# Where the matrix engine's tiles begin in memory, and the order of the first two units' products

## The chip, the cores and the metric

The kernel runs on one core of one Trainium2 chip. The metric is the device time of one execution in microseconds (us), the median of 3 runs. TensorE (PE) multiplies, VectorE (DVE), ScalarE (ACT) and GpSimd (POOL) do the elementwise work, SyncE (SP) issues the transfers. PEld is TensorE's weight load, which runs beside its matmuls.

## The reference

Attention with a sigmoid in place of the softmax, then two feed-forward layers (the "mixtures"):

```
scores = scale * q @ k.T - log(S);  attn = 1 / (1 + exp(-scores));  x = attn @ v
x = reshape(x)                                  # 1792 tokens x 768
h = x @ w_in;  x = (h * cos(h)) @ w_out         # 768 -> 2048 -> 768
g = x @ w_gate;  v = x @ w_val                  # 768 -> 1536 each
out = (silu(g) * v) @ w_out2                    # 1536 -> 768
```

Four batches, 12 heads, 448 positions, head size 64. The weights come in as 64-bit floats.

## The kernel before

Everything is held transposed: 128 partitions are features, the free dimension is tokens, 448 at a time. Each operand of a mixture's product is split in two parts, a rounded one (`fp32r`) and what the rounding left, and a product is three matmuls, part by part (`THREE`).

**Attention** (`attention`, 24 pairs of heads): 24 matmuls for the scores (line 732), a sigmoid on ACT, 16 for the weighted values (line 746). Beside it the first weights are turned from 64-bit words to floats.

**The mixtures** are worked in units: a half of the tokens (`NH` = 2) by two blocks of 128 columns of the hidden layer. A unit has one sum of products in layer 1 and two (gate and value) in layer 2, 40 in all. Each such sum is seven products instead of eight (a Strassen-like form, `seven`), numbered 1 to 7; each is 9 matmuls of a 128x128 weight block with a 128x448 moving block (line 998). Then come the unit's down products: 6 steps of 12 matmuls (line 900). So there are 40 x 7 x 9 = 2520 up matmuls and 28 x 72 = 2016 down matmuls, 4536 in all. Layer 1 has 16 units (1008 up, 1152 down), layer 2 has 12 (1512 up, 864 down).

The order of the products is a string of tokens for each unit (lines 256 to 266): a digit is a product, `d` a down step of the unit before. `tokens(n, u)` hands it out. Product 1 opens a bank `a`; ACT copies it to bank `b` (`first_copy`, line 927); 6 adds into `a` and 2 into `b` after that; a second copy of `a`, after 6, goes to bank `e` (`second_copy`, line 932), and 7 and 3 wait for it.

The operands and their tiles:

- moving, up: `X[1], X[5], X[2], X[6]` stand in the tile `x0` (line 202), `X[7], X[3], X[4]` in `x1` (line 400), which takes the place of a pool that the attention had. `x0` and `x1` both read as `x` in the profile.
- moving, down: `g0` to `g3` (line 1062).
- weights: pairs of blocks `wa0, wa1` (line 215), `wb0` to `wb2` (line 1060) and one pair at the end of `x1` (line 402; in the profile it reads as `x` too), and single blocks `s` (line 216).

A moving block is 448 x 4 = 1792 bytes of a partition and a weight block 512; both are whole multiples of 128. So where a tile begins, counted past a multiple of 128 bytes, every block in it begins. In the built program these are: `x0` 0, `x1` 96, `g` 64, weights 64, the pair in `x1` 96. Attention's tiles begin at 64, `t` (the ring of raw weights) at 0, `u` (temporaries) at 64.

The order of the instructions on all engines is set by a planner in the kernel (`Order`, lines 74 to 147): each step has an assumed duration and a due time that comes from the token strings (lines 301 to 326), and the planner writes the steps down engine by engine. At run time every engine takes its list strictly in order.

Quoted lines:

```
THREE = ((0, 0), (0, 1), (1, 0))
FIRST = "1526734"
ONE = ("1526dd7d3d4dd", "15d2d6d7d3d4d")
TWO = "15d26d73d4"
```

Of the kernel before, what the change touches and what calls it, by code (L numbers as in the profile page):

```python
# [9 lines left out]
F32 = mybir.dt.float32  # L10
F32R = mybir.dt.float32r
# [139 lines left out]
def block_kernel(  # L151
# [12 lines left out]
    P = 128  # L164
# [6 lines left out]
    KH = KD // 2  # L171
# [2 lines left out]
    assert T == NH * 2 * N and B == 2 * NH and NP == KD and KD % 2 == 0  # L174
    NF1 = w_in.shape[0]
    NF2 = w_gate.shape[0]
    THREE = ((0, 0), (0, 1), (1, 0))
    ADD, SUB = ALU.add, ALU.subtract

# [7 lines left out]
    xp = ctx.enter_context(tc.tile_pool(name="xp", bufs=1))  # L187
# [7 lines left out]
    size, WT = KH * 2 * N, KD * P  # L195
    X = {}

    def give_x(tile, numbers):
        for a, i in enumerate(numbers):
            X[i] = tile[:, a * size:(a + 1) * size].rearrange("p (k m t) -> p k m t", k=KH, m=2)  # L200

    give_x(xp.tile([P, 4 * size], F32R, tag="x0", name="x0"), ORDER[:4])
    ring = xp.tile([P, 3, WT], F32, tag="t", name="t")
    sums = xp.tile([P, W], F32, tag="sum", name="sum")
    warm = xp.tile([P, 16], F32, tag="warm", name="warm")
    order = Order()
    free_t, raws, convs, pairs, singles, gslots, tmps, rounds, downbanks = (Slots(order) for _ in range(9))
    for a in range(2):
# [2 lines left out]
    def make_pairs(pool, n, name):  # L211
        for i in range(n):
            pairs.give(pool.tile([P, 2, 2, KH, P], F32R, tag=f"w{name}{i}", name=f"w{name}{i}"))
# [28 lines left out]

    NC = {1: NF1 // 2, 2: NF2 // 2}
    units = [(layer, h, c) for layer in (1, 2) for h in range(NH) for c in range(NC[layer])]
# [8 lines left out]

    PRODUCT = 0.203

    FIRST = "1526734"
    ONE = ("1526dd7d3d4dd", "15d2d6d7d3d4d")
    TWO = "15d26d73d4"
    LAST = ('1526d734', '15d26d73d4dd')

    def tokens(n, u):
        if n == 0:
            return FIRST
        if n == n_units - 1:
            return LAST[u]
        return TWO if units[n][0] == 2 else ONE[units[n - 1][2] % 2]
# [75 lines left out]
    scratch, ended = {}, []  # L342
    for w, n in ((w_in, NF1), (w_out, NF1), (w_gate, NF2), (w_val, NF2), (w_out2, NF2)):
        for f in range(n):
# [1 line left out]
            if w.dtype != U64:  # L346
                scratch[id(w), f][1].set()

    def stashed(n):
        return False  # L350

    def needs():

        def downs(n):
            if not (units[n][1] and stashed(n)):
                for k in range(2):
                    yield [(w_out if units[n][0] == 1 else w_out2, 2 * units[n][2], i, k) for i in range(2)]

        for n, (layer, h, c) in enumerate(units):
            if not (h and stashed(n)):  # L360
                for w in (w_in,) if layer == 1 else (w_gate, w_val):
                    for i in range(2):
                        yield [(w, 2 * c, i, None)]
                    if n and w in (w_in, w_gate):
                        yield from downs(n - 1)
            elif n:
                yield from downs(n - 1)
        yield from downs(n_units - 1)
# [17 lines left out]
    def lend_pool():  # L386

        pool = tc.tile_pool(name="ln", bufs=1, side="right")
        ln, stop, backs = pool.__enter__(), [], []
        for a in range(4):  # L390
            raw = ln.tile([P, WT, 2], I32, tag=f"lr{a}", name=f"lr{a}")
            t = ln.tile([P, WT], F32, tag=f"lt{a}", name=f"lt{a}")
            backs.append(order.event())
            order.spawn(conversions(raw, t, backs[-1], stop), end)

        def swap():
            assert all(back.time is not None for back in backs)
            pool.__exit__(None, None, None)
            xr = ctx.enter_context(tc.tile_pool(name="xr", bufs=1, side="right"))
            x1 = xr.tile([P, 3 * size + 2 * WT], F32R, tag="x1", name="x1")  # L400
            give_x(x1, ORDER[4:])
            pairs.give(x1[:, 3 * size:].rearrange("p (m a k c) -> p m a k c", m=2, a=2, k=KH))
            x_open.set()

        return stop, swap
# [98 lines left out]
    def operands():  # L504
# [32 lines left out]
                stash[at][1].set()  # L537

        def stash_of(keys):
            n = keys[0][1] if keys[0][0] == "d" else keys[0][0]  # L540
            layer, h, c = units[n]
            return h, stashed(n), (layer, c) + (keys[0][2:] if keys[0][0] != "d" else ("d", *keys[0][2:]))

        def again(keys, size):

            room = pairs if size == WT else singles
            s = yield room
            there, event = stash[stash_of(keys)[2]]
            yield event
            yield move(f32(s), there)  # L550
            done = order.event()
            users[id(s)] = len(keys)
            order.spawn(here(keys, s, room, done), 4)
# [21 lines left out]

        def downs(n):
            for k in range(2):
                if units[n][1] and stashed(n):
                    yield from again([("d", n, i, k) for i in range(2)], WT)
                else:  # L580
                    yield from down(n, k)

        def late(n):
            return tokens(n, 0).index("6") < tokens(n, 0).index("d")

        last_sums = None
        for n in range(n_units):
            if units[n][1] and stashed(n):
                yield from again([(n, 0, 1), (n, 0, 2)], WT)
                yield from again([(n, 0, 5)], W)  # L590
                if not late(n):
                    yield from downs(n - 1)
                yield from again([(n, 0, 6), (n, 0, 3)], WT)
                if late(n):
                    yield from downs(n - 1)
                yield from again([(n, 0, 7), (n, 0, 4)], WT)
                continue
            for u in range(units[n][0]):
                a0 = yield from take()
                a1 = yield from take()  # L600
                a11, a12, a21, a22 = a0[:, :W], a0[:, W:], a1[:, :W], a1[:, W:]
                first = yield from split([(n, u, 1), (n, u, 2)], a0)
                if last_sums:
                    yield last_sums
                yield combine(sums, a21, a22, ADD, due[n, u, 5] - 3.0)
                yield combine(a21, a11, a21, SUB, due[n, u, 7] - 3.0)
                last_sums = yield from split([(n, u, 5)], sums)
                yield first
                yield combine(a11, sums, a11, SUB, due[n, u, 6] - 4.0)
                yield combine(a12, a12, a11, SUB, due[n, u, 3] - 4.0)  # L610
                if n and u == 0 and not late(n):
                    yield from downs(n - 1)
                yield from split([(n, u, 6), (n, u, 3)], a0, a0)
                if n and u == 0 and late(n):
                    yield from downs(n - 1)
                yield from split([(n, u, 7), (n, u, 4)], a1, a1)
# [70 lines left out]
    def attention():  # L687
        with tc.tile_pool(name="at", bufs=2) as at:
# [36 lines left out]
            def scores(i, c):  # L725
# [3 lines left out]
                sc = banks[:, first:first + 2, :S]  # L729
                for n, (m, p) in enumerate(THREE):  # L730
                    for j, half in enumerate(heads):
# [147 lines left out]
    def down(n):  # L879
# [4 lines left out]
        for at, (j, d) in enumerate(steps):  # L884
# [10 lines left out]
            def do(_):  # L895
                for e in range(d, d + 2):
                    for i in range(2):
                        w, g = operand(("d", n, i, e // KH)), gs[n, i, j]
                        for m, p in THREE:
                            nc.tensor.matmul(  # L900
# [18 lines left out]
    def seven(n, u, turn, z, downs):  # L919
# [55 lines left out]
        for token in tokens(n, u):  # L975
# [18 lines left out]
            def do(_, i=i, bank=bank):  # L994
                w, x = operand((n, u, i)), X[i]
                for k in range(KH):
                    for m, p in THREE:
                        nc.tensor.matmul(  # L998
# [47 lines left out]
    with tc.manual_schedule():  # L1046
        nc.gpsimd.memset(warm, 0.0)
        for s in range(n_stages):
            order.spawn(inputs(s), 3.5)
        order.spawn(loads(), 3)  # L1050
        order.spawn(operands(), 4)
        order.spawn(banker(), 2)
        attention()
        with tc.tile_pool(name="mp", bufs=1) as mp:
            for i in range(2):
                raws.give(mp.tile([P, WT, 2], I32, tag=f"raw{i}", name=f"raw{i}"))
                order.spawn(conversions(), end)
            convs.give(mp.tile([P, WT], F32, tag="cv", name="cv"))
            convs.give(ring[:, 2])
            make_pairs(mp, 3, "b")  # L1060
            for i in range(4):
                gslots.give(mp.tile([P, 2, N], F32R, tag=f"g{i}", name=f"g{i}"))
            for i in range(6):
                (tmps if i < 5 else rounds).give(mp.tile([P, N], F32, tag=f"u{i}", name=f"u{i}"))
            free_t.give(mp.tile([P, WT], F32, tag="t3", name="t3"))
            order.spawn(tensor_engine(), 0)
            order.run()
            assert not order.open
# [51 lines left out]
```

## Time and profile before

| | |
|---|---|
| time, median of 3 runs | 1100.19 us (1099.14 to 1101.25) |
| the profiled execution's own time | 1099.62 us |
| its span | 1097.8 us |
| instructions | 14763 |
| PE busy | 1080.3 us, 98% |
| PEld busy | 933.7 us, 85% |
| DVE busy | 849.6 us, 77% |
| ACT busy | 663.5 us, 60% |
| POOL busy | 126.4 us, 12% |
| DMA | 156.68 MB, mean 143 GB/s |

The profiled execution took 1099.62 us, of which 1.8 lie around the span. Busy time of PE says little of how fast it goes: a matmul's record lasts longer than the distance to the next one. What a matmul costs is the distance of the starts. In the timeline a row is a group of alike instructions; the start of the next row less its own start, over the count, is the mean distance.

### The profile page before, as it was taken

What the parts mean: (1) busy time and instruction counts of PE and PEld (TensorE: products, weight loads), DVE (VectorE), ACT (ScalarE), POOL (GpSimd) and SP (SyncE); (2) the same over time, 40 slices, a digit from 0 to 9 for tenths busy, and PEclk for the clock granted to TensorE, in tenths of its full rate; (3) what the DMA queues carried; (4) which work ended last, traced back from release to release, by engine and by line L of the source; (5) the groups of instructions that cost most, each with busy time, mean ns of one, the idle gap of its engine ahead of it and who ended that gap; (6) DMA issues with size and microseconds to landing.
All of it is one profiled execution on the core that took longest, in us unless ns stands there. A gap on an engine that the chain in (4) does not pass through costs nothing.

```text
span 1097.8 us, 14763 instructions
## 1 busy us (share of the span) xinstructions
PE 1080.3 (98%) x5507; PEld 933.7 (85%) x5507; DVE 849.6 (77%) x1139; ACT 663.5 (60%) x1002; POOL 126.4 (12%) x99
## 2 busy tenths in 40 slices
PE   9999999999999899999998999999999999999998
PEld 5555569999998799999997999999999999999997
DVE  4979759888999988988899888887559634655643
ACT  6888768776777777777776565544335444433330
POOL 0100001111211101100023111111111110110100
PEclk9999999999999999999998999999999999999999
DMA  9999334455644155544514566555122322212002
GB/s 268 303 284 234 120 116 148 170 181 185 222 162 139 45 188 187 187 144 158 179 52 144 177 207 212 179 193 168 37 65 75 133 66 73 59 43 72 29 1 101
DMA packets 64455, 156.68 MB, mean 143 GB/s; under 512 B 10112, under 2 KB 36736, under 8 KB 64384
## 3 DMA queue, kind: packets, MB, share of 16 engines
q1 hardware_dynamic: 64240, 155.51, 44.3%
q8 instruction: 43, 0.70, 0.3%
q10 hardware_dynamic: 144, 0.23, 0.1%
q14 instruction: 28, 0.23, 0.1%
HBM read 123.47 MB, written 32.24 MB: 142 GB/s over the span
## 4 chain that ended last, share of the span: by engine, by line
PE 89%; DVE 8%; ACT 1%; issue 1%; DMA 0%; DVEq 0%; ACTq 0%
PE banks L998 42%; PE banks L900 34%; PE banks L746 7%; PE banks L732 6%; DVE r L228 2%; DVE x L228 2%; DVE u L228 1%; DVE g L228 1%; DVE wb L228 1%; DVE u L814 1%; DMA rqk<-in_qk 0%; DVE wa L228 0%; ACT u L225 0%; DVE t L433 0%; DVE x L658 0%
## 5 line engine op out<-in xcount | busy, mean ns | idle before, releaser
L900 PE MATMUL banks<-g,wb 128*128 128x448 f32 x1044 | 228.5, 367 | 0.5 <-DVE g L228 0.4
L998 PE MATMUL banks<-x,wb 128*128 128x448 f32 x1044 | 228.9, 367 | 0.0
L998 PEld LDWEIGHTS banks<-x,wb 128*128 128x128 f32 x1044 | 197.2, 189 | 17.4 <-ACT banks L225 0.3
L900 PEld LDWEIGHTS banks<-g,wb 128*128 128x128 f32 x1044 | 196.0, 188 | 18.3 <-DVE g L228 1.1
L900 PE MATMUL banks<-g,wa 128*128 128x448 f32 x720 | 162.7, 373 | 9.8 <-ACT g L225 8.0
L998 PE MATMUL banks<-x,wa 128*128 128x448 f32 x738 | 162.7, 367 | 0.0
L900 PEld LDWEIGHTS banks<-g,wa 128*128 128x128 f32 x720 | 137.4, 191 | 23.7 <-ACT g L225 9.2
L998 PEld LDWEIGHTS banks<-x,wa 128*128 128x128 f32 x738 | 138.5, 188 | 13.0 <-issue 0.7
L225 ACT ACTIVATE u<-u 128x448 f32<-128x448 f32 x179 | 99.8, 571 | 44.2 <-DVE u L228 26.8
L228 DVE TENSOR_TENSOR u<-u,banks 128x448 f32<-128x448 f32 x119 | 73.3, 617 | 65.5 <-PE banks L998 60.5
L228 DVE TENSOR_TENSOR r<-banks,r 128x896 f32<-128x896 f32 (+1 forms) x69 | 74.2, 1075 | 53.5 <-PE banks L900 53.1
L736 ACT ACTIVATE a<-banks 128x896 f32<-128x896 f32 x96 | 82.9, 920 | 19.5 <-PE banks L732 12.0
L228 DVE TENSOR_TENSOR wb<-t,wb 128x768 fp32r<-128x768 f32 x73 | 69.3, 955 | 14.0 <-ACT wb L225 13.4
L225 ACT ACTIVATE g<-u 128x448 fp32r<-128x448 f32 x97 | 55.1, 573 | 40.9 <-DVE u L228 23.5
L998 PE MATMUL banks<-x,s 128*128 128x448 f32 x360 | 79.3, 364 | 0.0
L225 ACT ACTIVATE wb<-t 128x768 fp32r<-128x768 f32 x73 | 60.7, 837 | 25.3 <-PE banks L998 17.7
L732 PEld LDWEIGHTS banks<-qk 64*128 64x128 f32 x576 | 51.7, 189 | 27.7 <-ACT lr L225 8.5
L225 ACT ACTIVATE r<-banks 128x896 f32<-128x896 f32 x52 | 47.8, 920 | 41.6 <-PE banks L900 41.3
L510 POOL TENSOR_TENSOR sum<-t 128x384 f32<-128x384 f32 x20 | 34.1, 1704 | 333.8 <-DMA t<-swi 93.0
L998 PEld LDWEIGHTS banks<-x,s 128*128 128x128 f32 x360 | 67.6, 188 | 5.2
L732 PE MATMUL banks<-qk 64*128 64x448 f32 x576 | 69.8, 386 | 2.0 <-ACT a L736 0.8
L225 ACT ACTIVATE banks<-banks 128x448 f32<-128x448 f32 x80 | 42.3, 528 | 46.0 <-PE banks L998 44.9
(103 smaller groups left out, 1476.4 us busy)
## 6 DMA issues: line engine op xcount, KB each, us to landing
raw<-in_w_out SPq DMA_DIRECT2D x23, 768.0 KB, 4.8
t<-swi SPq DMA_DIRECT2D x32, 384.0 KB, 3.7
t<-swo SPq DMA_DIRECT2D x64, 192.0 KB, 2.5
rqk<-in_qk SPq DMA_DIRECT2D x47, 224.0 KB, 7.6
raw<-in_w_gate SPq DMA_DIRECT2D x12, 768.0 KB, 4.6
raw<-in_w_val SPq DMA_DIRECT2D x12, 768.0 KB, 4.7
t<-swg SPq DMA_DIRECT2D x18, 384.0 KB, 3.1
t<-swd SPq DMA_DIRECT2D x34, 192.0 KB, 2.8
```

What stands on the lines that cost most here:

```text
L225: return {"ACT": time}, lambda _: nc.scalar.activation(**kw)
L228: return {"DVE": time}, lambda _: nc.vector.tensor_tensor(out=out, in0=in0, in1=in1, op=op)
L510: on.tensor_tensor(out=out, in0=a, in1=b, op=op)
L732: nc.tensor.matmul(sc[:, j], lhsT=both[half, m, 1, starts[c]:starts[c] + P], rhs=both[half, p, 0], start=n == 0, stop=n == 2,)
L736: nc.scalar.activation(out=a, in_=sc, func=AF.Sigmoid, bias=-math.log(S), scale=1.0 / math.sqrt(D))
L746: nc.tensor.matmul(o[half], lhsT=value, rhs=a[:, j], start=c == 0, stop=c == NCH)
L814: yield {"DVE": 0.62}, lambda _: nc.vector.scalar_tensor_tensor(out=u, in0=f, scalar=MAGIC, in1=u, op0=ALU.subtract, op1=ALU.subtract), ti ...
L900: nc.tensor.matmul(banks[:, first + e - d, :N], lhsT=w[:, m, e % KH, :], rhs=g[:, p], start=(i, m, p) == (0, 0, 0) and is_fresh and not pr ...
L998: nc.tensor.matmul(bank, lhsT=w[:, m, k, :], rhs=x[:, k, p, :], start=(k, m, p) == (0, 0, 0) and i in (1, 5), stop=(k, m) == (KH - 1, 1), ...
```

## The change

Three things. First, tiles move. `warm`, a scratch tile of 16 floats, becomes 24 floats (96 bytes) and is placed ahead of `x0`; a pad of 16 floats (64 bytes) takes its old place ahead of the weights, another stands between `wb2` and `g0`; `x1` grows by 32 floats and its weight pair starts 16 floats further in. After it all of `x0`, `x1` and `g` begin 96 bytes past a multiple of 128, and all weight tiles 32 past one. Attention's tiles come to 32, `t` and `u` to 96.

Second, the first two units' token strings: the first unit goes 1 5 6 2 7 3 4 (was 1 5 2 6 7 3 4), the second 1 5 6 2 7 d d 3 d d 4 d d (was 1 5 2 6 d d 7 d 3 d 4 d d).

Third, `stashed` gets a second argument and an empty list `KEPT`; it still says False for every unit, so that part adds no instruction.

```
@@ pools
+    warm = xp.tile([P, 24], F32, tag="warm", name="warm")
     give_x(xp.tile([P, 4 * size], F32R, tag="x0", name="x0"), ORDER[:4])
     ring = xp.tile([P, 3, WT], F32, tag="t", name="t")
     sums = xp.tile([P, W], F32, tag="sum", name="sum")
-    warm = xp.tile([P, 16], F32, tag="warm", name="warm")
+    xp.tile([P, 16], F32, tag="pad", name="pad")
@@ tokens
-    FIRST = "1526734"
+    FIRST = ("1562734", "15627dd3dd4dd")
...
-        if n == 0:
-            return FIRST
+        if n < 2:
+            return FIRST[n]
@@ stashed
-    def stashed(n):
-        return False
+    def stashed(n, kind):
+        return units[n][0] == 1 and kind in KEPT
@@ swap
-            x1 = xr.tile([P, 3 * size + 2 * WT], F32R, tag="x1", name="x1")
+            x1 = xr.tile([P, 3 * size + 2 * WT + 32], F32R, tag="x1", name="x1")
             give_x(x1, ORDER[4:])
-            pairs.give(x1[:, 3 * size:].rearrange("p (m a k c) -> p m a k c", m=2, a=2, k=KH))
+            pairs.give(x1[:, 3 * size + 16:3 * size + 16 + 2 * WT].rearrange("p (m a k c) -> p m a k c", m=2, a=2, k=KH))
@@ pool mp
             make_pairs(mp, 3, "b")
+            mp.tile([P, 16], F32, tag="pad", name="pad")
             for i in range(4):
                 gslots.give(mp.tile([P, 2, N], F32R, tag=f"g{i}", name=f"g{i}"))
```

What it moves in the order of instructions. PE, the first unit and the start of the second, before (a row is one product; the weight tile tells which):

```order
L998 MATMUL banks_63<-x0_66,wa0_70 128x448 x9
L998 MATMUL banks_63<-x0_66,s_72 128x448 x9
L998 MATMUL banks_63<-x0_66,wa0_70 128x448 x9
L998 MATMUL banks_63<-x0_66,wa1_71 128x448 x9
L998 MATMUL banks_63<-x1_1325 128x448 x9
```

and after (line 998 has become 1000):

```order
L1000 MATMUL banks_63<-x0_67,wa0_71 128x448 x9
L1000 MATMUL banks_63<-x0_67,s_73 128x448 x9
L1000 MATMUL banks_63<-x0_67,wa1_72 128x448 x9
L1000 MATMUL banks_63<-x0_67,wa0_71 128x448 x9
L1000 MATMUL banks_63<-x1_1326 128x448 x9
```

Product 6 (third row now, weights in `wa1`) has come ahead of product 2 (in `wa0`), so one product lies between 6 and 7, which waits for the copy that follows 6.

ACT, beside it, before (`banks<-banks` are the two copies; `u` and `wb` are temporaries and weights):

```order
L225 ACTIVATE banks<-banks 128x448
L225 ACTIVATE s<-sum 128x384
L225 ACTIVATE u_1443<-banks 128x448
L225 ACTIVATE u_1445<-banks 128x448
L225 ACTIVATE wb_1437<-t 128x768
L225 ACTIVATE u_1448<-u_1445 128x448
L225 ACTIVATE banks<-banks 128x448
```

and after:

```order
L227 ACTIVATE banks<-banks 128x448
L227 ACTIVATE s<-sum 128x384
L227 ACTIVATE u_1445<-banks 128x448
L227 ACTIVATE banks<-banks 128x448
L227 ACTIVATE wb_1438<-t 128x768
L227 ACTIVATE raw_1434<-raw_1434 128x768
```

The second copy has come ahead of a weight conversion and two temporaries. The new strings shift due times, so the planner orders ACT and DVE otherwise from here to about the last units of the first half of layer 1 (the first third of their lists). After that, and on PE outside the first two units, the lists are the same but for buffer numbers.

## Rows read from the trace of the kernel before

**Rows 1.** The page, parts 1 and 4: engines, and the chain's engines.
```profile
PE 1080.3 (98%) x5507; PEld 933.7 (85%) x5507; DVE 849.6 (77%) x1139; ACT 663.5 (60%) x1002; POOL 126.4 (12%) x99
PE 89%; DVE 8%; ACT 1%; issue 1%; DMA 0%; DVEq 0%; ACTq 0%
```
**Rows 2.** Stretches: length, busy us by engine (instructions), granted clock, DMA share, GB/s.
```profile
280.00:300.00 20.00, 19.76 (x97) 17.93 (x96) 19.93 (x29) 15.10 (x25) 6.10 (x4) 1.00 0.63 209
360.00:370.00 10.00, 6.78 (x29) 5.68 (x28) 10.00 (x16) 7.81 (x15) 0.00 (x0) 0.93 0.28 83
575.00:595.00 20.00, 14.78 (x73) 13.31 (x71) 20.00 (x23) 15.03 (x24) 3.16 (x1) 0.97 0.24 79
610.00:850.00 240.00, 240.00 (x1177) 220.80 (x1176) 192.66 (x255) 119.39 (x180) 36.34 (x28) 1.00 0.45 149
```
**Rows 3.** Waits of PE: us in total, times, longest us.
```profile
PE banks L900 <- ACT g L225: 8.0, 3, 5.2
```
**Rows 4.** Timeline of PE, a unit of layer 1: start us, us, instructions.
```profile
194.36 1.98 PE L998 MATMUL banks<-x,s 128*128 128x448 f32 x9
196.18 2.63 PE L900 MATMUL banks<-g,wb 128*128 128x448 f32 x12
198.65 1.98 PE L998 MATMUL banks<-x,x 128*128 128x448 f32 x9
...
207.24 2.00 PE L998 MATMUL banks<-x,wb 128*128 128x448 f32 x9
209.08 2.59 PE L900 MATMUL banks<-g,wb 128*128 128x448 f32 x12
211.50 2.02 PE L998 MATMUL banks<-x,wa 128*128 128x448 f32 x9
213.36 2.60 PE L900 MATMUL banks<-g,wb 128*128 128x448 f32 x12
```
**Rows 5.** Timeline of PE, a unit of layer 2.
```profile
703.00 1.97 PE L998 MATMUL banks<-x,x 128*128 128x448 f32 x9
704.80 2.64 PE L900 MATMUL banks<-g,wb 128*128 128x448 f32 x12
...
717.04 1.98 PE L998 MATMUL banks<-x,s 128*128 128x448 f32 x9
718.86 2.64 PE L900 MATMUL banks<-g,wa 128*128 128x448 f32 x12
721.34 3.80 PE L998 MATMUL banks<-x,wb 128*128 128x448 f32 x18
724.98 1.39 PE L900 MATMUL banks<-g,wa 128*128 128x448 f32 x6
...
727.43 2.02 PE L998 MATMUL banks<-x,wa 128*128 128x448 f32 x9
729.28 2.02 PE L998 MATMUL banks<-x,wb 128*128 128x448 f32 x9
731.14 2.61 PE L900 MATMUL banks<-g,x 128*128 128x448 f32 x12
```
**Rows 6.** Weight loads from `wa`, 702 to 745 us: duration ns min/median/max.
```profile
L900 PEld LDWEIGHTS banks<-g,wa x25: 187/188/189, 712.0 to 745.0; 128*128 128x128 f32 x25
```
**Rows 7.** Timeline of DVE: two weight splits, into `x1`'s pair and into `wb`.
```profile
586.11 0.95 DVE L228 TENSOR_TENSOR x<-t,x 128x768 fp32r<-128x768 f32 x1
586.97 0.95 DVE L228 TENSOR_TENSOR wb<-t,wb 128x768 fp32r<-128x768 f32 x1
```
**Rows 8.** Timeline of PE, then of ACT, in the first unit.
```profile
154.94 3.80 PE L998 MATMUL banks<-x,wa 128*128 128x448 f32 x18
159.36 2.09 PE L998 MATMUL banks<-x 128*128 128x448 f32 x9 [0.62 <-ACT banks L225]
...
157.40 0.84 ACT L225 ACTIVATE wb<-t 128x768 fp32r<-128x768 f32 x1
158.78 0.53 ACT L225 ACTIVATE banks<-banks 128x448 f32<-128x448 f32 x1
```

More of the change, by code (lines that the diff above doesn't have):

```diff
@@ L176, in block_kernel @@
     NF2 = w_gate.shape[0]
+    KEPT = ()
     THREE = ((0, 0), (0, 1), (1, 0))
@@ L347, in block_kernel @@
                 scratch[id(w), f][1].set()
-    def stashed(n):
-        return False
+    def stashed(n, kind):
+        return units[n][0] == 1 and kind in KEPT
     def needs():
         def downs(n):
-            if not (units[n][1] and stashed(n)):
+            if not (units[n][1] and stashed(n, "down")):
                 for k in range(2):
@@ L359, in needs @@
         for n, (layer, h, c) in enumerate(units):
-            if not (h and stashed(n)):
+            if not (h and stashed(n, "up")):
                 for w in (w_in,) if layer == 1 else (w_gate, w_val):
@@ L539, in stash_of @@
         def stash_of(keys):
-            n = keys[0][1] if keys[0][0] == "d" else keys[0][0]
+            kind, n, at = ("down", *keys[0][1:2], keys[0][2:]) if keys[0][0] == "d" else ("up", keys[0][0], keys[0][1:])
             layer, h, c = units[n]
-            return h, stashed(n), (layer, c) + (keys[0][2:] if keys[0][0] != "d" else ("d", *keys[0][2:]))
+            return h, stashed(n, kind), (kind, layer, c, *at)
         def again(keys, size):
@@ L577, in downs @@
             for k in range(2):
-                if units[n][1] and stashed(n):
+                if units[n][1] and stashed(n, "down"):
                     yield from again([("d", n, i, k) for i in range(2)], WT)
@@ L587, in operands @@
         for n in range(n_units):
-            if units[n][1] and stashed(n):
+            if units[n][1] and stashed(n, "up"):
                 yield from again([(n, 0, 1), (n, 0, 2)], WT)
```

## The prediction, made before the changed kernel ran

> **What bounds the kernel now.** I read the page's engines and chain first, then the stretches, then the waits, then PE's timeline row by row. PE is busy 98% of the span and 89% of the chain that ended last is PE's [rows 1]. So the kernel takes as long as PE's matmuls do, plus the few places where PE waits. In the reader's eye two things should stay: a long stretch of layer 2 where PE never rests, 240.00 of 240 us [rows 2], and three stretches of layer 1 in which DVE is busy all the time (19.93 of 20, 10.00 of 10, 20.00 of 20 us) while PE has gaps [rows 2]. The second and third lie at the ends of the two halves of layer 1; there PE waits for `g`, 8.0 us in three waits, the longest 5.2 [rows 3]. So layer 2 is PE's alone, and layer 1 is PE's with DVE close behind.
>
> **What a matmul costs.** Every mixture matmul has the same size, 128x128 with 128x448, at the full clock, and yet their distances differ by the tile that moves. In the layer 2 unit `x0` with weights at 64 takes (718.86 - 717.04) / 9 = 202.2 ns a matmul and (724.98 - 721.34) / 18 = 202.2; `x1` takes (731.14 - 727.43) / 18 = 206.1; `g` takes (721.34 - 718.86) / 12 = 206.7 [rows 5]. In the layer 1 unit `x0` takes 1.82 / 9 = 202.2 again, `x1` 1.84 / 9 = 204.4 and 1.86 / 9 = 206.7, `g` 2.47 / 12 = 205.8 and 2.42 / 12 = 201.7 [rows 4]. One `x0` row is lower still: with the weight pair that lies in `x1` it takes 1.80 / 9 = 200.0 [rows 5]. A weight load lasts 187 to 189 ns [rows 6], so the distance is a load plus 11 to 19 ns, and it is this rest that differs. Neither partitions, columns nor type differ between the rows. What differs is which tile is read, and so where it begins. That is evidence, not proof: `g` and `x` also stand at different places in a unit.
>
> Means of these rows: `x0` 202.2; `x1` (1.84 + 1.86 + 3.71 us) / 36 = 205.8; `g` (2.47 + 2.42 + 2.48) / 36 = 204.7.
>
> **The change part by part.**
>
> *Where tiles begin.* Written as (moving, weights) past a multiple of 128, before has `x0` (0, 64), `g` (64, 64) and `x1` (96, 64), each with a few at weights 96. After it every mixture matmul is (96, 32). No row shows that pair, so its price is bounded by the nearest ones: 200.0 ns below, 206.7 ns above. I take 202.2, the price of (0, 64): it is the row whose distance between the two starts is the same, 64 of 128, and it is also the most regular one (the same 202.2 in all the `x0` rows with `wa`, `wb` or `s`). The choice rests on the distance being what matters, which the trace supports only weakly: (64, 64), distance 0, is 204.7, and (96, 64), distance 32, is 205.8, but (0, 96), distance 32 too, is 200.0.
>
> At 202.2 for all: `x1`, products 7, 3, 4, is 40 x 3 x 9 = 1080 matmuls, each 3.6 ns less, 3.9 us. `g` is 2016 matmuls, each 2.5 ns less, 5.0 us. `x0`, 1440, stays, but for those with the pair in `x1` (one pair in six, about 200), which lose 2.2 ns each, 0.4 us.
>
> Not all of it arrives. In layer 2 (648 of `x1`, 864 of `g`: 2.3 + 2.2 = 4.5 us) PE waits for nobody in a long stretch, so I count it whole. In layer 1 (432 and 1152: 1.6 + 2.9 = 4.5 us) DVE works through before both ends [rows 2]; where PE comes earlier, it waits longer for `g`. I count half, 2.2 us; the ends are none and all.
>
> *Attention's tiles* go from 64 to 32, moving and weights alike. Distance 0 stays, so I cost it at nothing. Bound: 288 pairs of score matmuls and 384 passes for the values are 672 streams; at the 3.6 ns between `x1` and `x0` that is 2.4 us either way.
>
> *DVE, ACT and POOL* read and write shifted tiles as well. A split into the pair at 96 and one into `wb` at 64 take 0.95 us alike [rows 7], so nothing.
>
> *The first two units.* Before, 18 matmuls of products 2 and 6 begin at 154.94; at 202.2 ns they are through at 158.58, and product 7 begins at 159.36, held by the second copy, which ACT begins at 158.78, behind a weight conversion of 0.84 us [rows 8]. After, product 6 is the third, so the copy has product 2's 1.8 us to run in, and in ACT's list it stands ahead of the conversion. That takes away 159.36 - 158.58 = 0.8 us. In the second unit product 7 comes before the first down steps instead of after two of them; the count of products is the same, and the `g` that those steps need are made one product later while the steps come one product later: nothing. What is late next is product 3's or 4's copy, which has a product or more in between.
>
> *The planner's other order* of ACT and DVE up to the last units of the first half of layer 1 moves work on a DVE that is full there. The first wait for `g`, at the end of that half, can grow or shrink. The nearest price is that wait itself: 10.00 - 6.78 = 3.2 us of PE's idle time in that stretch [rows 2]. I take 0, with 3 us either way. `stashed` adds no instruction.
>
> Sum: 4.5 + 2.2 - 0.4 + 0.8 = 7.1 us less than the profiled execution's 1099.6, so 1092.5; the median of the three runs stands 0.6 above that execution, within their spread. I say **1092.5 us**. Its own range, with layer 1's part whole or nothing and the order's 3 us, is 1088 to 1097.
>
> **The rivals.**
>
> *The moving tile's start alone decides* (the other side). By start the rows go up: 0 is 202.2, 64 is 204.7, 96 is 205.8. Then (96, 32) is the worst of them, `x0` loses 3.6 ns a matmul and `g` 1.1. Layer 2: 864 x 3.6 + 864 x 1.1 = 4.1 us; layer 1: 576 x 3.6 + 1152 x 1.1 = 3.3 us, half of which its waits take up, 1.7. Less 0.8 for the first unit: 1104.6; with attention's 2.4, 1107. At 206.7 for all, and no wait that takes any up, it is 1440 x 4.5 + 2016 x 2.0 + 1080 x 0.9 = 11.5 us, 1110. For it: the order of the three is even, and the two starts are tied to tiles in the trace, so the distance rule fits no better. Against it: `x0` with two weight starts gives 202.2 and 200.0, so the weights' start matters too. It decides as soon as products 1, 5, 2, 6 come above 205 ns.
>
> *The new pair is as good as the best row*, 200.0 ns. Then layer 2's 2376 matmuls give 2.2 ns more each, 5.2 us, and layer 1's 2160 half of 4.8: 1092.5 - 7.6 = 1084.9. With layer 1's part whole it is about 1080. For it: a row at 200.0 exists, and one pair in the whole program lets the three kinds of product stop alternating. Against it: it is one tile's row.
>
> *The starts don't matter*, and the rows differ for what stands beside them in a unit. Then only the first unit's 0.8 us is left: 1098.8, no change that can be told. The Trainium skill says this in effect ("TensorE: Matmul & The Clock Gate", Part 2: What happens when you issue a matmul): TensorE has separate SBUF read ports for the moving operand and the weights, so loading the next weights takes nothing from the running matmul; by its spacing of the columns over 2.4 GHz plus about 2.5 ns a matmul of 448 columns would be 189 ns whatever its address. The trace does not bear the figure out: no row is below 200.0.
>
> **How the numbers follow.** The forecast gets 0.35, the better pair 0.27, the slower rival 0.25, no effect 0.13. A measurement of this kernel can tell about 0.2%, 2.2 us, from no change; the forecast and the better pair lie below that (0.62), the third rival inside (0.13), the slower one above (0.25). The range reaches from 1080, the better pair with layer 1 whole, to 1107, the slower one with attention; it leaves out a tenth at either end.
>
> **What would show it.** In the changed kernel's timeline of PE a product (9 matmuls) of `x0`, of `x1` and a down step per 9 matmuls should all be 1.82 us apart. 1.85 or more for the first four products is the slower rival, 1.80 or less for all the better pair, 1.82, 1.85 and 1.84 by tile as before the third. The wait of product 7 in the first unit should be gone. At the end of layer 1 PE's wait for `g` should be longer than 5.2 us if PE became faster and DVE didn't, and about as long if the starts don't matter. A total beyond 1080 to 1107, or attention's pairs of heads some tenths of a us longer, would prove the prediction wrong in a way none of the cases holds.

## The result, and the profile after

The changed kernel takes 1090.1 us (median of 6 runs, 1086.72 to 1093.96) against 1099.24 us for the kernel before (6 runs, 1097.62 to 1101.25): a ratio of 0.9914 with a 95% interval of 0.9891 to 0.9938. It is faster by about 9 us. The forecast was 1092.5 us in a range of 1080 to 1107. The profiled execution took 1090.07 us, its span 1087.9.

The page of the kernel after, parts 1 and 4, answers to [rows 1]: PE is busy 12.8 us less (1080.3 to 1067.5), and PE's share of the chain fell from 89% to 86%, with 2% of DMA that was not there.

```profile
PE 1067.5 (98%) x5507; PEld 930.7 (86%) x5507; DVE 846.4 (78%) x1138; ACT 664.3 (61%) x1005; POOL 126.4 (12%) x97
PE 86%; DVE 9%; DMA 2%; issue 1%; ACT 1%; SPq 1%; DVEq 0%; ACTq 0%
```

The stretches of the kernel after, with the columns of [rows 2], and one of attention:

```profile
100.00:120.00 20.00, 17.85 (x114) 9.44 (x112) 19.26 (x24) 13.84 (x17) 0.00 (x0) 0.91 0.78 187
360.00:370.00 10.00, 6.40 (x26) 5.28 (x25) 10.00 (x16) 7.75 (x15) 0.19 (x1) 0.89 0.29 84
575.00:595.00 20.00, 14.33 (x64) 12.58 (x63) 19.88 (x24) 13.37 (x21) 6.40 (x1) 0.87 0.35 113
610.00:850.00 240.00, 239.89 (x1193) 223.34 (x1192) 195.20 (x259) 120.67 (x182) 36.92 (x29) 1.00 0.45 148
```

In the 240 us of layer 2 PE does 1193 matmuls where it did 1177; it is as full as before and each matmul takes less. At the two ends of layer 1's halves it rests a little more. PE's wait for `g`, which answers to [rows 3], went from 8.0 us in three waits (longest 5.2) to:

```profile
PE banks L902 <- ACT g L227: 8.9, 3, 5.6
```

PE's timeline of the kernel after, a unit of layer 1, then one of layer 2, answers to [rows 4, 5]:

```profile
209.11 1.96 PE L1000 MATMUL banks<-x,wb 128*128 128x448 f32 x9
210.91 2.56 PE L902 MATMUL banks<-g,wb 128*128 128x448 f32 x12
213.31 1.96 PE L1000 MATMUL banks<-x,wa 128*128 128x448 f32 x9
215.11 2.56 PE L902 MATMUL banks<-g,wb 128*128 128x448 f32 x12
...
698.16 1.97 PE L1000 MATMUL banks<-x,x 128*128 128x448 f32 x9
699.96 2.56 PE L902 MATMUL banks<-g,wb 128*128 128x448 f32 x12
...
712.02 1.98 PE L1000 MATMUL banks<-x,s 128*128 128x448 f32 x9
713.84 2.57 PE L902 MATMUL banks<-g,wa 128*128 128x448 f32 x12
716.25 3.80 PE L1000 MATMUL banks<-x,wb 128*128 128x448 f32 x18
719.89 1.37 PE L902 MATMUL banks<-g,wa 128*128 128x448 f32 x6
...
722.31 1.97 PE L1000 MATMUL banks<-x,wa 128*128 128x448 f32 x9
724.11 1.96 PE L1000 MATMUL banks<-x,wb 128*128 128x448 f32 x9
725.91 2.59 PE L902 MATMUL banks<-g,x 128*128 128x448 f32 x12
```

Read them as distances of starts. In layer 1 `x1` is (210.91 - 209.11) / 9 = 200.0 ns and `g` 2.40 / 12 = 200.0. In layer 2 `x1` is (725.91 - 722.31) / 18 = 200.0, but `x0` is still (719.89 - 716.25) / 18 = 202.2, as in [rows 5]; with the pair in `x1` it is 1.80 / 9 = 200.0. So two of the three moving tiles dropped by 4 to 6 ns a matmul to the level of the best row of before, and the third did not move.

**The account.** Span by stage in the two profiled executions, from the starts in PE's timelines: the first mixture product starts at 151.20 before and 154.71 after; from there to the end of the last matmul are 943.1 and 929.7 us; behind it 3.5 and 3.5. So the mixtures gave 13.4 us and attention took 3.5 back, 9.9 in the span. Where layer 1 ends, at the wait for `g`, the first fence is before, the second after:

```profile
587.48 1.98 PE L998 MATMUL banks<-x,s 128*128 128x448 f32 x9
594.69 5.25 PE L900 MATMUL banks<-g,wa 128*128 128x448 f32 x12 [5.22 <-ACT g L225]
```

```profile
584.27 1.98 PE L1000 MATMUL banks<-x,s 128*128 128x448 f32 x9
591.89 5.04 PE L902 MATMUL banks<-g,wa 128*128 128x448 f32 x12 [5.64 <-ACT g L227]
```

The ninth matmul ahead of that wait starts 1.62 us into its row: layer 1 up to there took 589.10 - 151.20 = 437.9 us before and 585.89 - 154.71 = 431.2 after, 6.7 less; the rest 505.2 and 498.6, 6.6 less. Both layers gave the same, though DVE is full at the ends of layer 1's halves.

By kind of matmul, the mean distance of starts over the whole trace (distances of 230 ns and more left out: these are waits, and stretches at the lower of TensorE's two clock levels, 1.2 GHz, as in `g`'s row behind the wait above, which lasts 5.04 us where 2.56 is usual), and what each gave; the counts are the means of the two traces:

| moving, weights | matmuls | before ns | after ns | us |
|---|---|---|---|---|
| `x1` with `wa`, `wb`, `s` | 918 | 205.5 | 200.1 | -5.0 |
| `x1` with the pair | 162 | 204.4 | 202.1 | -0.4 |
| `g` with `wa`, `wb` | 1733 | 204.2 | 200.3 | -6.7 |
| `g` with the pair | 252 | 203.9 | 202.2 | -0.4 |
| `x0` with `wa`, `wb`, `s` | 1214 | 202.2 | 202.35 | +0.2 |
| `x0` with the pair | 216 | 201.9 | 200.2 | -0.4 |

These make -12.7 us, and -12.8 when the 40 or so left out are counted at the mean of their kind. What the waits and the stretches at 1.2 GHz add beyond that went from 18.4 to 17.9 us. Together this is the 13.4.

### The profile page after: what moved, and what is told of

It reads as the page before. It is cut to its first block, busy times and chain, and to the rows that moved or that the text cites. A ratio compares the mean times of both kernels' runs of the same rounds, so it can differ in the third digit from the quotient of the medians.

```text
span 1087.9 us, 14759 instructions
## 1 busy us (share of the span) xinstructions
PE 1067.5 (98%) x5507; PEld 930.7 (86%) x5507; DVE 846.4 (78%) x1138; ACT 664.3 (61%) x1005; POOL 126.4 (12%) x97
## 4 chain that ended last, share of the span: by engine, by line
PE 86%; DVE 9%; DMA 2%; issue 1%; ACT 1%; SPq 1%; DVEq 0%; ACTq 0%
PE banks L1000 42%; PE banks L902 33%; PE banks L748 6%; PE banks L734 5%; DVE x L230 2%; DVE r L230 2%; DMA rqk<-in_qk 2%; DVE u L230 1%; DVE g L230 1%; DVE wa L230 1%; DVE wb L230 0%; DVE u L816 0%; DVE s L230 0%; DVE x L660 0%; SPq L707 0%
## 5 line engine op out<-in xcount | busy, mean ns | idle before, releaser
L902 PE MATMUL banks<-g,wb 128*128 128x448 f32 x1044 | 224.5, 363 | 1.1 <-ACT g L227 0.5
L1000 PE MATMUL banks<-x,wb 128*128 128x448 f32 x1044 | 225.0, 363 | 0.1
L902 PE MATMUL banks<-g,wa 128*128 128x448 f32 x720 | 159.9, 369 | 9.9 <-ACT g L227 8.4
L512 POOL TENSOR_TENSOR sum<-t 128x384 f32<-128x384 f32 x20 | 36.6, 1832 | 339.7 <-DMA t<-swi 147.3
```

What stands on the lines that cost most here:

```text
L512: on.tensor_tensor(out=out, in0=a, in1=b, op=op)
L902: nc.tensor.matmul(banks[:, first + e - d, :N], lhsT=w[:, m, e % KH, :], rhs=g[:, p], start=(i, m, p) == (0, 0, 0) and is_fresh and not pr ...
L1000: nc.tensor.matmul(bank, lhsT=w[:, m, k, :], rhs=x[:, k, p, :], start=(k, m, p) == (0, 0, 0) and i in (1, 5), stop=(k, m) == (KH - 1, 1), ...
```

## The experiments

The reading after the result: the price follows from how far the moving block begins behind the weight block, counted modulo 256 bytes and not 128. Before, `x0` stood 192 behind its weights, `g` 0 and `x1` 32; after, `x0` still 192, but `g` and `x1` 64. Rivals: the order of products gave the time; the places themselves, not the distance, decide; attention's shift took part of it back.

The kernels from strings_only to places_b in the table ran on one chip. Since attention's length varied from execution to execution, this table sets the profiled execution's time beside the start of the first mixture product; their difference is the mixtures' part. "Mean ns" is the mean distance of starts of the mixtures' matmuls, and "by distances" is 948.4 (the kernel before) plus 4536 times its change.

| kernel | mean ns | execution us | first product at | difference | by distances |
|---|---|---|---|---|---|
| before | 203.82 | 1099.62 | 151.20 | 948.4 | |
| strings_only | 203.80 | 1098.32 | 149.68 | 948.6 | 948.3 |
| after | 201.00 | 1090.07 | 154.71 | 935.4 | 935.6 |
| places_only | 201.00 | 1087.93 | 151.09 | 936.8 | 935.6 |
| attn64 | 201.00 | 1089.67 | 153.63 | 936.0 | 935.6 |
| all64 | 200.01 | 1084.38 | 152.00 | 932.4 | 931.1 |
| av64 | 200.01 | 1083.19 | 149.91 | 933.3 | 931.1 |
| qk64 | 200.01 | 1085.46 | 152.75 | 932.7 | 931.1 |
| places_a | 204.51 | 1100.97 | 151.63 | 949.3 | 951.5 |
| places_b | 203.21 | 1095.11 | 150.07 | 945.0 | 945.6 |

The last two columns differ by up to 2.2 us, for the most part through waits and stretches at 1.2 GHz. These come to 15.9 us in places_a, 17.6 in places_b, 17.9 to 19.7 in the kernels with 201.0 ns, against 18.4 before and 18.5 in strings_only, and to 19.4 to 20.3 in the three with 200.01. So at most 1.9 us of what the faster matmuls gave went into more waiting.

### The change in two halves: strings_only and places_only

strings_only is the kernel before with the new order alone:

```
-    FIRST = "1526734"
+    FIRST = ("1562734", "15627dd3dd4dd")
-        if n == 0:
-            return FIRST
+        if n < 2:
+            return FIRST[n]
```

> Before with only the first two units' new token strings; all tiles stand where they stood. Theory (the places of the tiles carry nearly all of the gain): 0.8 us under before, ratio 0.9993, product 7 of the first unit no longer waits, and the distances of the matmuls stay as before (x0 202.2, x1 204 to 207, g 202 to 207 ns). Rival (the planner's other order is worth something by itself): 2 us or more under before, ratio 0.998 or lower, with shorter waits for g in the first half of layer 1.

Measured: 1099.35 us (12 runs) against 1098.87 (17), ratio 1.0000 (0.9990 to 1.0011). Its timeline of PE in the first unit, and later in layer 1, then a row of the kernel before:

```profile
153.43 3.80 PE L998 MATMUL banks<-x,wa 128*128 128x448 f32 x18
157.07 2.02 PE L998 MATMUL banks<-x 128*128 128x448 f32 x9
...
304.50 0.47 PE L900 MATMUL banks<-g,wb 128*128 128x448 f32 x1 [0.55 <-ACT g L225]
305.29 2.50 PE L900 MATMUL banks<-g,wb 128*128 128x448 f32 x11 [0.33 <-DVE g L228]
```

```profile
283.62 1.69 PE L900 MATMUL banks<-g,wb 128*128 128x448 f32 x7 [0.24 <-DVE g L228]
```

Product 7 now starts 3.64 us behind the 18 matmuls ahead of it, 18 x 202.2 ns: the wait of [rows 8] is gone. But the planner's other order makes new waits at 304 us, 0.55 and 0.33. Before has no wait there; it has one at 283 us (0.24). In distances of starts the new pair is 1.3 us beyond the cadence, the old one 0.5, the first unit's 0.8: nothing is left over.

places_only is the changed kernel with the old order put back (the same lines the other way).

> The change without its new token strings: only the tiles are moved. Theory: the distances of the changed kernel (x0 with wa, wb, s 202.3 ns; x0 with the pair in x1 200.2; x1 and g 200.2, with the pair in x1 202.2) and about 8 us under before, ratio 0.993; product 7 of the first unit waits as before. Rival (the strings carry a part): 5 us or less under before, ratio 0.9955 or higher.

Measured: 1088.29 us (5 runs), ratio 0.9908 (0.9889 to 0.9927), and the same 201.00 ns. The whole gain is the places'; the order gives nothing that 0.1% would show.

### Attention's tiles put back: attn64

In the changed kernel, ahead of attention's first tile:

```
+            at.tile([P, 8], F32, tag="pad", name="pad", bufs=1)
```

> The changed kernel with a pad of 32 bytes ahead of attention's tiles, so that they begin 64 past a multiple of 128 as before the change, and all else stands as in it. Theory (transfers into tiles that begin at 32 go slower, so that attention waits for them): the first product of the mixtures starts at 151 us as before, not at 155, and the time is 3 us under the changed kernel, about 1087, ratio to before 0.989. Rival (attention's waits differ from one execution to the next whatever the tiles): the same time as the changed kernel within 1 us.

Measured: 1087.38 us (5 runs), ratio 0.9887 (0.9866 to 0.9907). The first mixture product starts at 153.63, late as in the changed kernel (154.71) though attention's tiles begin at 64 again, while places_only, with attention's tiles at 32, has 151.09. So the late start doesn't go with the tiles' places. It goes with one wait of PE for ACT's `a` near 103 us. First before, then after, then attn64:

```profile
102.83 0.88 PE L732 MATMUL banks<-qk 64*128 64x448 f32 x6 [0.84 <-ACT a L736]
```

```profile
104.76 1.28 PE L734 MATMUL banks<-qk 64*128 64x448 f32 x6 [2.15 <-ACT a L738]
```

```profile
103.60 0.88 PE L735 MATMUL banks<-qk 64*128 64x448 f32 x6 [2.17 <-ACT a L739]
```

In both late kernels a stretch at 1.2 GHz follows this rest of PE: the mean granted clock of 100 to 120 us is 0.91 in after (the first stretch above) and in attn64, where before has 1.00:

```profile
100.00:120.00 20.00, 19.16 (x134) 10.66 (x136) 19.86 (x26) 16.55 (x21) 0.00 (x0) 1.00 0.55 147
```

In the other profiled executions of the table the clock is 1.00 there, and the start goes by the same wait. There is none in strings_only, av64 and places_b (149.68 to 150.07), 0.66 to 0.99 us in places_only, before and places_a (151.09 to 151.63), 1.61 in all64 (152.00) and 2.38 in qk64 (152.75). What makes `a` late is not shown. DVE's waits for the transfers of `qk` are longer too, first before, then after (total us, times, longest), but no run here tells whether the one comes from the other:

```profile
DVE qk L721 <- DMA rqk<-in_qk: 12.4, 5, 4.8
```

```profile
DVE qk L723 <- DMA rqk<-in_qk: 19.4, 8, 5.4
```

Whether the changed kernel's attention is longer on average these runs don't settle.

### Every mixture distance at 64: all64

Weights first in the pool, pads sized so that `x0`, `g` and `x1` begin at 192 past a multiple of 256 and every weight tile at 128:

```
-    warm = xp.tile([P, 24], F32, tag="warm", name="warm")
+    warm = xp.tile([P, 16], F32, tag="warm", name="warm")
...
-    xp.tile([P, 16], F32, tag="pad", name="pad")
...
-            x1 = xr.tile([P, 3 * size + 2 * WT + 32], F32R, tag="x1", name="x1")
-            give_x(x1, ORDER[4:])
-            pairs.give(x1[:, 3 * size + 16:3 * size + 16 + 2 * WT].rearrange("p (m a k c) -> p m a k c", m=2, a=2, k=KH))
+            x1 = xr.tile([P, 3 * size + 2 * WT + 24], F32R, tag="x1", name="x1")
+            give_x(x1[:, 2 * WT + 16:], ORDER[4:])
+            pairs.give(x1[:, :2 * WT].rearrange("p (m a k c) -> p m a k c", m=2, a=2, k=KH))
...
+            mp.tile([P, 48], F32, tag="pad", name="pad")
```

The tiles `wa` and `s` have moved ahead of `x0`, and the pairs `wb` behind `g` and that last pad; the changed kernel's pad ahead of `g` is gone.

> Another placing of all tiles, with the change's strings: weights at 128 of 256 bytes (all of them, the pair in x1 too), x0, x1 and g at 192 of 256, attention's tiles at 64 of 128 as before the change. Theory (what counts is the distance from the weights' start to the moving tile's, modulo 256; 64 is the good one): 200.2 ns for every kind of product, x0 too, so 1.5 to 3.5 us under the changed kernel for that, and about 1085 with attention as before. Rival one (the distance counts modulo 128): x0 stays at 202.3. Rival two (the moving tile's own start counts modulo 128; here it is 64, where g took 204.7 before the change): 204 to 205 ns for all, and 1100 or more.

Measured: 1084.73 us (4 runs), ratio 0.9873 (0.9854 to 0.9893). PE's timeline of all64, layer 2:

```profile
708.25 1.96 PE L998 MATMUL banks<-x,s 128*128 128x448 f32 x9
710.05 2.56 PE L900 MATMUL banks<-g,wa 128*128 128x448 f32 x12
712.45 3.76 PE L998 MATMUL banks<-x,wb 128*128 128x448 f32 x18
716.05 1.36 PE L900 MATMUL banks<-g,wa 128*128 128x448 f32 x6
...
720.25 1.96 PE L998 MATMUL banks<-x,wb 128*128 128x448 f32 x9
722.05 2.56 PE L900 MATMUL banks<-g,x 128*128 128x448 f32 x12
```

1.80 us for nine, 2.40 for twelve, 3.60 for eighteen: 200.0 ns in every row, whatever the tile and the place in the unit. The moving tiles begin here where `g` began before, with its 204.2 ns, so the place of the moving tile by itself does not decide the price. The difference to the changed kernel is 4536 x 1.0 = 4.5 us by distances, 2.1 to 3.0 us in the table (932.4, 933.3 and 932.7 against 935.4); the two ratios' intervals just touch. all64 is faster than the kernel before by far more than the interval, and no layout tried here is faster than all64 beyond the intervals.

### Other distances: places_a and places_b

The same arrangement as all64 with other pads. places_a sets `x0` 96, `g` 128 and `x1` 80 behind the weights; places_b 112, 160 and 48:

```
places_a:
+    warm = xp.tile([P, 24], F32, tag="warm", name="warm")
...
+            give_x(x1[:, 2 * WT + 20:], ORDER[4:])
...
+            mp.tile([P, 8], F32, tag="padg", name="padg")
...
+            mp.tile([P, 32], F32, tag="pad", name="pad")
places_b:
+    warm = xp.tile([P, 24], F32, tag="warm", name="warm")
+    give_x(xp.tile([P, 4 * size + 8], F32R, tag="x0", name="x0")[:, 4:4 + 4 * size], ORDER[:4])
...
+            give_x(x1[:, 2 * WT + 12:], ORDER[4:])
...
+            mp.tile([P, 8], F32, tag="padg", name="padg")
...
+            mp.tile([P, 24], F32, tag="pad", name="pad")
```

> As all64, with three other distances from the weights' start to the moving tile's, modulo 256, that no run has shown: x0 at 96, x1 at 80, g at 128. If the distance alone counts, each tile has one price, whichever it is. Theory (64 is the best): all three dearer than 200.0 ns, g at 128, half of 256, the dearest, about 203 to 206. Rival (any distance that isn't near 0 is as good): 200.0 to 200.5 for all three.

> As all64, with distances x0 112, x1 48, g 160. The two 16-byte steps show how fine the rule is. Theory (64 is the best, and 160 has been seen before, 200 to 202 for the few products that had it): x1 at 48 between 200 and 205.6, x0 at 112 between 200 and 206, g at 160 201.5 to 202.5. Rival (only whole 32-byte steps count): x1 at 48 as it was at 32, 205.5, or as at 64, 200.0.

Measured, one run each: 1100.97 and 1095.11 us, beside 1099.0 for the kernel before. PE's timeline in layer 2, places_a first, then places_b:

```profile
718.15 2.61 PE L900 MATMUL banks<-g,wa 128*128 128x448 f32 x12
720.60 3.86 PE L998 MATMUL banks<-x,wb 128*128 128x448 f32 x18
724.29 1.37 PE L900 MATMUL banks<-g,wa 128*128 128x448 f32 x6
```

```profile
714.96 2.58 PE L900 MATMUL banks<-g,wa 128*128 128x448 f32 x12
717.38 3.86 PE L998 MATMUL banks<-x,wb 128*128 128x448 f32 x18
721.08 1.38 PE L900 MATMUL banks<-g,wa 128*128 128x448 f32 x6
```

`x0`, the cheap tile of before at 202.2, is now (724.29 - 720.60) / 18 = 205.0 and (721.08 - 717.38) / 18 = 205.6; `g` is 2.45 / 12 = 204.2 and 2.42 / 12 = 201.7. The tile has lost its rank with its distance: neither the tile nor its place in the unit alone decides. Every price here is above 200.0, but 128 is not the dearest distance: the dear ones are 32, 96 and 112. The table of all distances seen, from the means over whole traces:

| distance, bytes mod 256 | ns | where |
|---|---|---|
| 0 | 204.2, 204.4 | before: `g`; `x1` with the pair |
| 32 | 205.5 | before: `x1` |
| 48 | 203.0 | places_b: `x1` |
| 64 | 200.0 to 200.3 | after: `g`, `x1`, `x0` with the pair; all64, av64, qk64: all |
| 80 | 204.8 | places_a: `x1` |
| 96 | 205.3 | places_a: `x0` |
| 112 | 205.9 | places_b: `x0` |
| 128 | 203.7 | places_a: `g` |
| 160 | 201.9, 201.5 | before: `x0` with the pair; places_b: `g` |
| 192 | 202.2, 202.35, 202.2, 202.1 | before: `x0`; after: `x0`; after: `g` and `x1` with the pair |
| 224 | 203.9 | before: `g` with the pair |

Equal distances at unlike places cost alike: 192 with `x0` at 128 (before) and at 224 (after), 64 with moving tiles at 96 and 192.

These are means over a kind, and away from 64 something besides the distance acts within them. In places_a, `x1` with `wa`, `wb` and `s`, all at 80, takes 203.7 ns in layer 1 and 205.7 in layer 2. In places_b, `g` is at 160 throughout, yet the first six matmuls of a down step take 202.9 ns and the last six 200.0. At 64, in all64, every kind takes 200.0 in both layers. What acts there stays open, so the order of the dear distances among themselves is not to be leaned on.

### Attention's own distances: av64 and qk64

all64 with attention's operands shifted, for the weighted values:

```
+            at.tile([P, 16], F32, tag="pad", name="pad", bufs=1)
```

and for the scores, where `q`'s and `k`'s parts lie in one tile:

```
-                both = at.tile([P, 2, 2, S], F32R, tag="qk", name=f"qk{i}")
+                row = 2 * S + 64
+                both = at.tile([P, 2 * row - 48], F32R, tag="qk", name=f"qk{i}")
+                both = [[both[:, m * row + (S + 16) * (1 - j):][:, :S] for j in range(2)] for m in range(2)]
```

(qk64 splits `q` and `k` by one instruction each where all64 takes both in one.)

> As all64, with the probabilities of attention 64 bytes further, so that the values' matmuls (moving: probabilities, weights: values) have the distance 64 where they had 0. Theory (their weight load has 64 columns and is short, so the stream of the moving tile is the limit, not the load): their group of 16 stays at 3.16 us and the time at 1084.7. Rival (the distance helps every matmul): 16 matmuls in 3.0 us, 24 groups, 3 to 4 us under all64.

> As all64, with q and k apart in attention's tile, so that the scores' matmuls have the distance 64 where they had 0; their split is done in four DVE operations instead of two for that. Theory (two loads of 64 rows each for two streams at a time: the loads are the limit here, and the distance acts as in the mixtures): 24 matmuls in about 2.70 instead of 2.76 us, 1 to 1.5 us in all, at most what the added DVE operations cost. Rival: no change in the 2.76.

Measured: 1083.58 us (4 runs), ratio 0.9859 (0.9841 to 0.9876), and 1084.57 (4 runs), 0.9868 (0.9849 to 0.9888); neither differs from all64 beyond the intervals. PE's timeline in attention, all64 first, then av64 and qk64:

```profile
113.53 2.82 PE L732 MATMUL banks<-qk 64*128 64x448 f32 x24
116.28 2.48 PE L746 MATMUL banks<-a,vs 128*64 128x448 f32 x12
...
119.44 2.82 PE L732 MATMUL banks<-qk 64*128 64x448 f32 x24
```

```profile
114.20 2.48 PE L746 MATMUL banks<-a,vs 128*64 128x448 f32 x12
...
117.36 2.82 PE L732 MATMUL banks<-qk 64*128 64x448 f32 x24
```

```profile
114.24 2.83 PE L736 MATMUL banks<-qk 64*128 64x448 f32 x24
117.00 2.48 PE L750 MATMUL banks<-a,vs 128*64 128x448 f32 x12
```

The 16 matmuls for the values take 119.44 - 116.28 = 3.16 us in all64 and 117.36 - 114.20 = 3.16 in av64; the 24 for the scores take 2.75 in all64 and 2.76 in qk64. In attention 64 is worth no more than 0; other distances were not tried there.

### Own weights or the next ones: parts32

While a block moves, the weights of the next matmul are loaded: PEld and PE have 5507 instructions each and are busy side by side, 86% and 98% of the span in the kernel after. In all kernels so far the distance to a block's own weights and to the next ones is the same, but for the seams between products, so the table holds for both together. parts32 is all64 with the second part of `x` and of every weight tile (which the down products share) set 32 bytes further from the first, while `g` stays. Now the two distances differ. To make room it has one buffer of raw weights and one `vs` buffer less, so its time says nothing.

```
+    SHIFT = 8
+
+    def parted(tile, n):
+        return tile[:, :2 * n + 2 * SHIFT].rearrange("p (m r) -> p m r", m=2)[:, :, :n]
...
-            free_t.give(mp.tile([P, WT], F32, tag="t3", name="t3"))
```

> As all64, but in the up products' operands the second part (what the rounding left) stands 32 bytes further than the first, in x and in the weights alike; one buffer of raw weights and one of attention's values less, to make room. Of three matmuls of an up product, the distance from a matmul's own weights to its moving block is 64, 96, 32; the distance from the weights that are loaded beside it, the next matmul's, to its moving block stays 64, 64, 64. Theory (it is the next weights' load, running beside the moving block's stream, that the distance acts on): up products stay at 200.0 ns. Rival (a matmul's own two operands count): 200.0, 205.3 and 205.5 in turn, or 203.6 in the mean. The time itself says nothing here, since the loads have a buffer less.

Measured: 1345.51 us (one run), with 262 us of waits and stretches at 1.2 GHz. Where PE is full, its timeline reads:

```profile
716.39 2.00 PE L1007 MATMUL banks<-x,wb 128*128 128x448 f32 x9
718.23 2.00 PE L1007 MATMUL banks<-x,s 128*128 128x448 f32 x9
720.07 2.61 PE L909 MATMUL banks<-g,wa 128*128 128x448 f32 x12
```

An up product is 1.84 / 9 = 204.4 ns a matmul. By kind over the whole trace, up products: own distance 64, 202.6 ns; 96, 206.0; 32, 206.5; with the distance to the weights loaded next 64 throughout. That the next load's distance alone counts would make all three 200.0, and that falls. Own distance puts them in the order of the table, but each is 0.7 to 2.6 ns above it. The down products say the opposite: `g` at 64 from its own weights is 202.9 with the next ones at 64 and 206.2 with them at 32, and at 32 from its own with the next at 64 it is only 202.3, below the table's 205.5 for 32. There the next weights' distance orders the prices. So neither distance alone explains all six; both take part, or a matmul's price depends on its neighbours' too. This stays open.

## Why the prediction was right, and where its steps failed

**What bounds it** held: PE's matmuls, one shorter by some ns, carry the whole result; 12.7 of the 13.4 us in the mixtures are distances of starts.

**What decides a matmul's price** was right in kind (the distance of the two starts) and wrong in period. The prediction took the distance between the two starts, modulo 128, and set (96, 32) equal to (0, 64), 202.2 ns. Modulo 256 these are two cases: `x0` stays at 192, its 202.35 ns as forecast, while `g` and `x1` go to 64, where a matmul takes 200.1 to 200.3. The row that the prediction found odd, `x0` with the pair at 200.0, is `x0` of one unit; over the trace of before that kind is 201.9, at 160.

**The terms.** For `x1` 3.9 us were forecast and 5.4 came; for `g` 5.0 and 7.1 (the table of kinds). `x0` with the pair was to lose 0.4 and gave 0.4. So the forecast held for the third of the matmuls in which `x0` moves, less the pair, and the rival of the better pair for most of the rest. The other `x0` lost 0.2. This is the mis-sized step: 3.9 + 5.0 - 0.4 = 8.5 us at full count were 12.7.

**Layer 1's half** was wrong. Of its gain 2.2 us were struck off for waits; layer 1 gave 6.7 us, as much as layer 2, and the longest wait for `g` grew only from 5.2 to 5.6 us. Waits and stretches at 1.2 GHz took at most 1.9 us more than before in any of the faster kernels (20.3 in av64 against 18.4), and none in the changed one. The work in front of that wait depends on PE's earlier products, so when PE is early through the half, most of what it waits for is early too. That last sentence is argued from the two waits and not tested by itself.

**The first unit** gave its 0.8 us, and the planner's order, which the prediction set at 0 with 3 us either way, took it back at 304 us (strings_only).

**Attention** at nothing was right as to the tiles (attn64, av64, qk64). But the changed kernel's profiled execution had 3.5 us more of attention, and its median is near that execution. So it is partly luck that the forecast of 7.1 us is near the measured 9: the matmuls gave 4.2 us more than forecast at full count and the 2.2 us struck off layer 1 came as well, and attention's late start hid 3.5 of that.

**The rivals.** That the moving start alone decides falls by all64: moving tiles at 64 past a multiple of 128, all at 200.0, where the rule gave 204.7. That starts don't matter falls by places_only against strings_only, and by places_a, whose `x0` went to 205.3. The Trainium skill ("TensorE: Matmul & The Clock Gate", Part 2: What happens when you issue a matmul) lets the weight load take no read bandwidth from the running matmul; no run here shows what is shared, but 200.0 to 205.9 ns by where the two operands begin does not agree with operands whose places never matter to each other.

## What to carry to other kernels

Where matmuls of one shape differ by a few ns in the trace, list the mean distance of starts by moving tile and weight tile beside each tile's start in the built program, before looking for waits; here about 1% of the whole kernel lay in the padding. For 128x128 with 128x448 `fp32r` blocks, set the moving block 64 bytes past its weights modulo 256, both parts of each operand alike, and check every pair, the odd buffer too. Test a layout rule with layouts in which tile and distance part company, and compare executions stage by stage, since an unrelated stretch can vary by as much as the effect.

## What the hardware showed that was not expected

- The mean price of a matmul goes with the distance of its two starts modulo 256 bytes and not smoothly: 200.0 ns at 64, 203.0 at 48, 204.8 at 80, 205.9 at 112, 203.7 at 128, 202.2 at 192.
- At 64 the weight load is no shorter; [rows 6] has 187 to 189 ns, and in the kernel after (702 to 745 us) they are:

```profile
L902 PEld LDWEIGHTS banks<-g,wa x36: 187/188/191, 707.0 to 741.9; 128*128 128x128 f32 x36
```

- Attention's matmuls, 64 rows or 64 columns of weights, cost the same at 0 and at 64 (3.16 us for 16, 2.75 and 2.76 for 24).
- With the two parts of `x` and of the weights 32 bytes further apart, five of the six kinds were dearer than the table has them by their own distance, by 0.7 to 6.2 ns, and `g` at 32 was 3.2 ns cheaper (parts32).
